# Backward pass of single-query attention: products by streaming evicted blocks past zero-padded columns, scores turned by transposes

## The chip, the cores and the metric

The kernel runs on one core of a Trainium2 chip. A core has TensorE (PE in the profile, with its weight loads as PEld), VectorE (DVE), ScalarE (ACT), GpSimd (POOL) and SyncE (SP), and 16 DMA engines that move data between HBM and the on-chip memories SBUF and PSUM. The metric is the device time of one execution in microseconds (us), as the median of several runs.

## The reference

For each of 2 x 32 = 64 heads there is one query row q of 128 elements, 8192 key rows and 8192 value rows of 128 elements, all bf16. The function returns the attention output and the gradients of q, k and v for a given grad_out:

```python
def _fwd_reference(q, k, v):
    scale = q.shape[-1] ** -0.5
    scores = jnp.einsum("bhqd,bhkd->bhqk", q, k) * scale
    p = _softmax(scores, axis=-1)
    return jnp.einsum("bhqk,bhkd->bhqd", p, v)
...
    _out, _vjp = jax.vjp(_f, q, k, v)
    _grads = _vjp(grad_out)
```

Written out for one head: s = K q, P = softmax(scale s), out = P V, dP = V grad_out, dS = P (dP - sum(P dP)), dq = scale dS K, dK = scale dS q^T, dV = P grad_out^T. K and V (2 MB each) are read once, dK and dV (2 MB each) are written once.

## The kernel before, in words

K and V of a head lie in SBUF as tiles kt and vt of 128 partitions by 64 blocks of 128 elements: partition p holds 64 consecutive tokens. Five heads have buffers at a time. dV is computed in place over vt, dK over kt, and both are stored from there.

The order of all work is written out by hand (`manual_schedule`, L353 to L399): each engine executes its instructions in program order. A pass of the loop over h works on two heads: y, head h, whose scores are computed, and x, head p = h - 1, whose sums and outer products follow. A pass has eight stages j, each with two halves u. Stages 0 to 3 go over K's blocks of head h, stages 4 to 7 over V's.

- `transposes` (L106): per half, eight PE transposes (matmuls against an identity, L113) put eight 128x128 blocks into one of two PSUM buffers tp; one instruction evicts them to SBUF as ev, on ACT (L120), or on DVE (L118) in the second halves of stages 0 and 7.
- `products` (L124): per half, eight matmuls with an ev block as weights and the one column q (or grad_out) of the head as the moving operand (L136). Each gives 128 scores in a column of `sm` (or `dp`). Products of a half stand one stage behind its transposes.
- `row_max`, `all_max`, `exps` (L158 to L182): the maximum over all scores, through one small PE transpose and a broadcasting matmul, and E = exp(...) on ACT.
- `deltas`, `sums`, `weights` (L191 to L232): the sums of E and of E dP, by a matmul with ones, and from them the weights of the outer products, on DVE.
- `weighted_rows` (L234): the sums over tokens for out and dq, as matmuls of 32 weight columns against 512 streamed elements, four at a time on four column groups of PE (`tile_position`, L241). Eight zero-padded weight tiles wz, one for each of four heads and both sums, place a head's result in its own rows of `acc`; every fourth head `acc_to_sbuf` and `combine` read it.
- `outer` (L266): eight DVE multiplications a head (L271) write dV and dK in place; `store` (L328) issues the 2 MB stores from ACT's queue at stages 4 and 7, and `load` (L97) the loads from SP's queue. One store in 26 goes out in pieces through POOL's queue (L289). The last head's stores are four pieces of 1 MB.

The schedule around the change reads:

```python
            for j in range(NS):
                for u in range(2):
                    if y:
                        transposes(h, j, u)
...
                    if y and j:
                        products(h, j - 1, u)
                    elif x and j == 0:
                        products(p, NS - 1, u)
                    if x and j < 4:
                        weighted_rows(p, j // 2, (2 * (j % 2) + u,))
```

Of the kernel before, what the change touches and what calls it, by code (L numbers as in the profile page):

```python
# [23 lines left out]
def kernel(  # L24
# [34 lines left out]
    for g in range(1, 4):  # L59
# [21 lines left out]
    qT_all = const.tile([P, BH], BF16)  # L81
    doT_all = const.tile([P, BH], BF16)


    rl_all = const.tile([P, 2, BH], F32)

    wz = [
        [const.tile([P, NT // 4, 32], BF16, name=f"wz{w}{k}") for k in range(OG)]
        for w in range(2)
    ]  # L90
    colsT = const.tile([P, 2, BH], BF16)
# [5 lines left out]
    def load(h):  # L97
        x = heads[h]
        x.kv = [
            kvp.tile([P, NT, D], BF16, name="kt", tag="kt"),  # L100
            kvp.tile([P, NT, D], BF16, name="vt", tag="vt"),
        ]
        for dst, src in zip(x.kv, (k_v, v_v)):
            nc.sync.dma_start(out=dst[:], in_=src[h])

    def transposes(h, j, u):  # L106

        x = heads[h]
        w, c = divmod(j, NS // 2)
        tp = ps_tp.tile([P, HC, P], F32, name="tp", tag="tp")  # L110
        for i in range(HC):
            n = c * CH + u * HC + i
            nc.tensor.matmul(  # L113
                tp[:, i, :], lhsT=x.kv[w][:, n, :], rhs=ident_bf[:], start=True, stop=True
            )
        ev = evp.tile([P, HC, P], BF16, name="ev", tag="ev")
        if u and j in (0, 7):
            nc.vector.tensor_copy(out=ev[:], in_=tp[:])  # L118
        else:
            nc.scalar.copy(out=ev[:], in_=tp[:])  # L120
        x.ev = getattr(x, "ev", {})
        x.ev[j, u] = ev

    def products(h, j, u):  # L124
        x = heads[h]
        w, c = divmod(j, NS // 2)
        if c == 0 and u == 0:
            if w:
                x.dp = ps_one.tile([P, NT + 2], F32, name="dp", tag="dp")
            else:  # L130
                x.sm = ps_one.tile([P, NT + P + 1], F32, name="sm", tag="sm")
        ev = x.ev.pop((j, u))
        col = (qT_all, doT_all)[w][:, h : h + 1]
        for i in range(HC):
            n = c * CH + u * HC + i
            nc.tensor.matmul(  # L136
                (x.dp if w else x.sm)[:, n : n + 1], lhsT=ev[:, i, :], rhs=col,
                start=True, stop=True,
            )

# [17 lines left out]
    def row_max(x):  # L158
        x.mp = work.tile([P, 1], F32, name="mp", tag="mp")
        nc.vector.reduce_max(out=x.mp[:], in_=x.sm[:, 0:NT], axis=AX.X)  # L160

    def all_max(x):
        mT = x.sm[0:1, NT : NT + P]
# [4 lines left out]
    def exps(x):  # L168
        mb = x.sm[:, NT + P : NT + P + 1]
# [6 lines left out]
            out=x.E[:],  # L176
            in_=x.sm[:, 0:NT],
# [6 lines left out]
    def to_weights(h, w, src):  # L184
        k = h % OG
        nc.vector.tensor_copy(  # L186
            out=wz[w][k][:, :, 16 * w + 4 * k : 16 * w + 4 * k + 4],
            in_=src[:].rearrange("p (m j) -> p m j", j=4),
        )

    def deltas(x):  # L191
        junk = work.tile([P, NT], BF16, name="junk", tag="junk")
        nc.vector.tensor_tensor_reduce(  # L193
            out=junk[:],
            in0=x.E[:],
            in1=x.dp[:, 0:NT],
# [7 lines left out]
    def sums(x):  # L204
        x.lsum = x.dp[:, NT : NT + 2]
        nc.tensor.matmul(x.lsum, lhsT=ones_f[:], rhs=x.ld[:], start=True, stop=True)  # L206

    def weights(h):
        x = heads[h]
        rl, rls = rl_all[:, 0, h : h + 1], rl_all[:, 1, h : h + 1]  # L210
        nc.vector.reciprocal(out=rl, in_=x.lsum[:, 0:1])  # L211
        negdelta = work.tile([P, 1], F32, name="negdelta", tag="negdelta")
        nc.vector.tensor_scalar(
            out=negdelta[:], in0=x.lsum[:, 1:2], scalar1=rl, scalar2=-1.0,
            op0=ALU.mult, op1=ALU.mult,
        )
        nc.vector.tensor_scalar(out=rls, in0=rl, scalar1=scale, scalar2=None, op0=ALU.mult)
        dSu = work.tile([P, NT], F32, name="dSu", tag="dSu")
        nc.vector.scalar_tensor_tensor(
            out=dSu[:], in0=x.dp[:, 0:NT], scalar=negdelta[:], in1=x.E[:],  # L220
            op0=ALU.add, op1=ALU.mult,
        )
        to_weights(h, 1, dSu)

        x.w2 = []
        for name, src, s in (("P2", x.E, rl), ("dS2", dSu, rls)):
            t = work.tile([P, NT, 2], BF16, name=name, tag=name)
            nc.vector.tensor_scalar(
                out=t[:], in0=src[:].unsqueeze(2).to_broadcast([P, NT, 2]),
                scalar1=s, scalar2=None, op0=ALU.mult,  # L230
            )
            x.w2.append(t)  # L232

    def weighted_rows(h, w, chunks):  # L234


        rows, k = heads[h].kv[1 - w], h % OG
        for c in chunks:
            for g in range(4):
                n = c * CH + 4 * g  # L240
                nc.tensor.matmul(  # L241
                    acc[32 * g : 32 * g + 32, :],
                    lhsT=wz[w][k][:, n // 4, :],
                    rhs=rows[:, n : n + 4, :].rearrange("p n d -> p (n d)"),
                    start=(w == 0 and k == 0 and c == 0),
                    stop=(w == 1 and k == OG - 1 and c == NT // CH - 1),
                    tile_position=(0, 32 * g),
                )
# [5 lines left out]
    def combine(h):  # L254

        x = heads[h]
        c = ps_one.tile([P, 2, OG], F32, name="c", tag="c")
        for j in range(4):
            nc.tensor.matmul(  # L259
                c[:], lhsT=x.accsb[:, j * D : (j + 1) * D], rhs=pick[:, j],  # L260
# [3 lines left out]
        nc.vector.tensor_mul(out=colsT[:, :, own], in0=c[:], in1=rl_all[:, :, own])  # L264
# [75 lines left out]
    spare = const.tile([16, 1024], BF16)  # L340
# [4 lines left out]
    for w in range(2):  # L345
        for t in wz[w]:
            nc.gpsimd.memset(t[:], 0.0)
    for src, dst in ((nat[:, 0, :], qT_all), (nat[:, 1, :], doT_all)):
        tps = ps_tp.tile([P, BH], BF16, name="tps", tag="tp")
        nc.tensor.transpose(tps[:], src, ident_bf[:BH, :BH])  # L350
        nc.vector.tensor_copy(out=dst[:], in_=tps[:])

    with tc.manual_schedule():  # L353
        for h in range(min(UNITS, BH)):
            load(h)
        for h in range(BH + 1):
# [4 lines left out]
            for j in range(NS):  # L361
                for u in range(2):
                    if y:
                        transposes(h, j, u)
                    if u == 0:
                        if x and j == 1:
                            sums(x)
                        if y and j == 5:
                            all_max(y)
                        if y and j == 6:  # L370
                            exps(y)
                    if y and j:
                        products(h, j - 1, u)
                    elif x and j == 0:
                        products(p, NS - 1, u)
                    if x and j < 4:
                        weighted_rows(p, j // 2, (2 * (j % 2) + u,))
                if x and j == 0:
                    deltas(x)
                if x and j == 1:  # L380
                    weights(p)
                if y and j == 4:
                    row_max(y)
                if y and j == 7:
                    to_weights(h, 0, y.E)
                if x and p < BH - 1 and j in (4, 7):
                    store(p, j // 7)
                if x:
                    for i in ((), (0,), (1, 2), (3, 4), (5,), (6,), (7,), ())[j]:
                        outer_and_store(p, i // 4, i % 4)  # L390
                    if full and j == 4:
                        acc_to_sbuf(x)
                    if full and j == 6:
                        combine(p)
                if j == 7:
                    if x and UNITS <= h + 3 < BH:
                        load(h + 3)
                    if y and h % QG == 0:
                        spread_rows(h // QG)  # L399
# [37 lines left out]
```

## Time and profile before

| what | value |
|---|---|
| median of 3 runs | 1285.84 us (1284.8 to 1286.18) |
| profiled execution, span | 1285.1 us |
| PE busy, weight loads PEld | 1060.3 us (83%), 877.3 us (68%) |
| DVE busy | 883.8 us (69%) |
| ACT busy | 909.3 us (71%) |
| POOL busy | 105.8 us (8%) |
| DMA | 539.69 MB, mean 420 GB/s |
| PE instructions | 18948 matmuls, 18948 weight loads |

The profile is of one execution, whose span is 1285.1 us; the device time of the runs includes a little around a span. Busy time is the time in which an engine executed something, with overlaps of pipelined matmuls counted once. A line of a group or of the timeline names the source line, the engine, the operation, the tile that is written and those that are read, their shape, and in brackets how long the engine had been idle and who released it. In a line of a stretch, the pairs are busy time and number of instructions of PE, PEld, DVE, ACT and POOL; then follow the clock granted to PE, the busy share of the DMA engines and GB/s. Timeline lines give start and length in us.

### The profile page before, as it was taken

What the parts mean: (1) busy time and instruction counts of PE and PEld (TensorE: products, weight loads), DVE (VectorE), ACT (ScalarE), POOL (GpSimd) and SP (SyncE); (2) the same over time, 40 slices, a digit from 0 to 9 for tenths busy, and PEclk for the clock granted to TensorE, in tenths of its full rate; (3) what the DMA queues carried; (4) which work ended last, traced back from release to release, by engine and by line L of the source; (5) the groups of instructions that cost most, each with busy time, mean ns of one, the idle gap of its engine ahead of it and who ended that gap; (6) DMA issues with size and microseconds to landing.
All of it is one profiled execution on the core that took longest, in us unless ns stands there. A gap on an engine that the chain in (4) does not pass through costs nothing.

```text
span 1285.1 us, 42433 instructions
## 1 busy us (share of the span) xinstructions
PE 1060.3 (83%) x18948; PEld 877.3 (68%) x18948; DVE 883.8 (69%) x1511; ACT 909.3 (71%) x1043; POOL 105.8 (8%) x193
## 2 busy tenths in 40 slices
PE   5999888848998799499997984999889849899983
PEld 4777777637777677477776774777767737777772
DVE  1887777737787486378875773787767636778775
ACT  5877778737887586488875774877767736788771
POOL 1000111000002110000021200000111000001120
PEclk9999999969999697799996897998979877999996
DMA  9999999999999999999999999999999999999998
GB/s 396 418 426 428 426 426 425 423 431 427 426 426 426 413 424 427 423 427 425 428 426 399 427 426 418 428 427 428 419 403 426 425 419 391 428 429 425 425 424 336
DMA packets 43879, 539.69 MB, mean 420 GB/s; under 512 B 10192, under 2 KB 10192, under 8 KB 10192
## 3 DMA queue, kind: packets, MB, share of 16 engines
q1 hardware_dynamic: 18432, 268.44, 49.5%
q10 hardware_dynamic: 18320, 258.02, 47.4%
q0 software_dynamic: 6944, 10.51, 2.2%
q8 instruction: 148, 2.42, 0.7%
q14 instruction: 35, 0.29, 0.1%
HBM read 268.47 MB, written 268.47 MB: 418 GB/s over the span
## 4 chain that ended last, share of the span: by engine, by line
PE 40%; DMA 26%; ACT 19%; DVE 11%; issue 3%; ACTq 0%; DVEq 0%; SPq 0%
PE tp L113 23%; ACT ev L120 18%; DMA vt<-in_v_dram 9%; DVE ev L118 9%; DMA out_dram<-vt 9%; PE acc L241 9%; DMA kt<-in_k_dram 4%; PE sm L136 4%; DMA out_dram<-kt 3%; PE dp L206 1%; PE dp L136 1%; PE c L259 1%; DMA nat<-in_grad_out_dram 1%; ACT E_f L175 1%; PE sm L170 1%
## 5 line engine op out<-in xcount | busy, mean ns | idle before, releaser
L120 ACT CAST ev<-tp 128x1024 bf16<-128x1024 f32 x896 | 881.2, 1024 | 335.7 <-PE tp L113 232.3
L113 PE MATMUL tp<-ident_bf,vt 128*128 128x128 bf16 x4096 | 327.4, 225 | 134.7 <-ACT ev L120 121.6
L113 PEld LDWEIGHTS <-vt 128*128 128x128 bf16 x4096 | 268.9, 100 | 167.3 <-issue 153.2
L113 PE MATMUL tp<-ident_bf,kt 128*128 128x128 bf16 x4096 | 335.9, 228 | 17.2 <-DMA kt<-in_k_dram 6.5
L113 PEld LDWEIGHTS <-kt 128*128 128x128 bf16 x4096 | 249.4, 101 | 131.5 <-issue 123.2
L136 PEld LDWEIGHTS <-ev 128*128 128x128 bf16 x8192 | 324.4, 98 | 2.2 <-issue 0.2
L271 DVE TENSOR_TENSOR kt<-qd,dS 128x2048 bf16<-128x2048 bf16 x256 | 310.0, 1212 | 0.0
L271 DVE TENSOR_TENSOR vt<-qd,P 128x2048 bf16<-128x2048 bf16 x256 | 295.8, 1216 | 0.0
L118 DVE CAST ev<-tp 128x1024 bf16<-128x1024 f32 x128 | 156.7, 1224 | 186.4 <-PE tp L113 179.4
L136 PE MATMUL dp<-doT_all,ev 128*128 128x1 bf16 x4096 | 178.5, 164 | 0.1
L136 PE MATMUL sm<-qT_all,ev 128*128 128x1 bf16 x4096 | 176.0, 164 | 0.0
L299 POOL DMA_DIRECT2D out_dram<-vt x120 | 67.0, 560 | 1032.7 <-DVE vt L271 832.1
L241 PE MATMUL acc<-vt,wz 128*32 128x512 bf16 x1024 | 109.3, 418 | 17.8 <-DVE wz L186 17.8
L241 PE MATMUL acc<-kt,wz 128*32 128x512 bf16 x1024 | 103.4, 396 | 0.1
L172 DVE TENSOR_SCALAR negm<-sm 128x1 f32<-128x1 f32 x64 | 9.8, 154 | 108.8 <-PE sm L170 108.8
L241 PEld LDWEIGHTS <-wz 128*32 128x32 bf16 x2048 | 52.8, 93 | 32.1 <-DVE wz L186 22.7
L285 POOL DMA_DIRECT2D spare<-in_q_dram x57 | 34.1, 598 | 121.1 <-DMA out_dram<-vt 107.0
L206 PE MATMUL dp<-ld,ones_f 128*128 128x2 f32 x128 | 25.8, 271 | 21.0 <-DVE ld L193 20.9
L206 PEld LDWEIGHTS dp<-ld,ones_f 128*128 128x128 f32 x128 | 20.6, 202 | 31.1 <-DVE ld L193 31.0
L160 DVE TENSOR_REDUCE mp<-sm 128x1 f32<-128x64 f32 x64 | 14.4, 225 | 36.9 <-PE sm L136 36.9
L211 DVE RECIPROCAL rl_all<-dp 128x1 f32<-128x1 f32 x64 | 10.7, 168 | 32.0 <-PE dp L206 32.0
L170 PE MATMUL sm<-gm,ones_f 1*128 1x1 f32 x128 | 25.8, 268 | 0.0
(42 smaller groups left out, 310.5 us busy)
## 6 DMA issues: line engine op xcount, KB each, us to landing
kt<-in_k_dram SPq DMA_DIRECT2D x64, 2048.0 KB, 22.9
vt<-in_v_dram SPq DMA_DIRECT2D x64, 2048.0 KB, 31.5
out_dram<-kt ACTq DMA_DIRECT2D x63, 2048.0 KB, 26.9
out_dram<-vt ACTq DMA_DIRECT2D x58, 2048.0 KB, 21.9
out_dram<-vt POOLq DMA_DIRECT2D x20, 176.0 KB, 23.2
out_dram<-vt POOLq DMA_DIRECT2D x40, 64.0 KB, 23.0
out_dram<-vt POOLq DMA_DIRECT2D x20, 128.0 KB, 22.6
out_dram<-vt ACTq DMA_DIRECT2D x2, 1024.0 KB, 10.9
```

Of the source, the lines that this page charges most:

```text
L113: nc.tensor.matmul(tp[:, i, :], lhsT=x.kv[w][:, n, :], rhs=ident_bf[:], start=True, stop=True)
L118: nc.vector.tensor_copy(out=ev[:], in_=tp[:])
L120: nc.scalar.copy(out=ev[:], in_=tp[:])
L136: nc.tensor.matmul((x.dp if w else x.sm)[:, n : n + 1], lhsT=ev[:, i, :], rhs=col, start=True, stop=True,)
L160: nc.vector.reduce_max(out=x.mp[:], in_=x.sm[:, 0:NT], axis=AX.X)
L170: nc.tensor.matmul(mb, lhsT=ones_f[0:1, :], rhs=x.gm[:], start=True, stop=True)
L175: nc.scalar.activation(out=x.E[:], in_=x.sm[:, 0:NT], func=ACT.Exp, bias=negm[:], scale=scale, accum_out=x.ld[:, 0:1],)
L206: nc.tensor.matmul(x.lsum, lhsT=ones_f[:], rhs=x.ld[:], start=True, stop=True)
L241: nc.tensor.matmul(acc[32 * g : 32 * g + 32, :], lhsT=wz[w][k][:, n // 4, :], rhs=rows[:, n : n + 4, :].rearrange("p n d -> p (n d)"), sta ...
L271: nc.vector.tensor_tensor(out=x.kv[1 - w][:, n : n + CH, :].rearrange("p n (d t) -> p n d t", t=2), in0=row.unsqueeze(1).to_broadcast([P, ...
L285: nc.gpsimd.dma_start(out=two(spare[0:n, :])[:, :, i : i + 2], in_=two(q_rows[0:n, :])[:, :, 0:2])
L299: nc.gpsimd.dma_start(out=dst[own], in_=src[own], max_dma_last_dim=size)
```

## The change

- The evicted blocks become the moving operand, and the column of q (or grad_out) the weights. Four matmuls a stage, one for each of PE's four column groups, each stream four blocks (512 elements) past four weight columns, three of which are zeros: q stands in column 3 of its four in `qz`, and the slice that is taken begins 3 - c columns to the left, so that the products of stage c land in row c of the group's four rows of `raw`, where four stages accumulate.
- So the products of both halves of a stage run together, once, behind the first half of the next stage.
- `raw` (512 scores in each of 16 rows) is copied to SBUF by DVE and turned by four fp32 transposes on PE into `turned`, where the scores stand by token again: for K at stages 4 and 5 of the head's own pass, for V at stages 0 and 1 of the next.
- The sum of E and the sum of E dP become two matmuls, the first at stage 7 of the head's own pass; `weights` splits into `weights_v` (stage 7) and `weights_k` (stage 1 of the next pass).
- One wz tile with 60 columns for each of the two sums takes the place of four with 32 columns; a shifted slice of it gives the head's rows.
- DVE evicts the second halves of stages 6 and 7, not of 0 and 7. Outer products, stores (stages 3 and 6), the second sum, `spread_rows` and `combine` move in the schedule.

The diff, cut to its core:

```diff
@@ transposes, products
-            n = c * CH + u * HC + i
+            n = CH * (2 * u + i // 4) + 4 * c + i % 4
...
-        if u and j in (0, 7):
+        if u and j in (6, 7):
             nc.vector.tensor_copy(out=ev[:], in_=tp[:])
         else:
             nc.scalar.copy(out=ev[:], in_=tp[:])
...
-    def products(h, j, u):
+    def products(h, j):
         x = heads[h]
         w, c = divmod(j, NS // 2)
...
-        ev = x.ev.pop((j, u))
-        col = (qT_all, doT_all)[w][:, h : h + 1]
-        for i in range(HC):
-            n = c * CH + u * HC + i
+        at = 4 * h + 3 - c
+        evs = [x.ev.pop((j, u)) for u in range(2)]
+        for k in range(4):
             nc.tensor.matmul(
-                (x.dp if w else x.sm)[:, n : n + 1], lhsT=ev[:, i, :], rhs=col,
-                start=True, stop=True,
+                raw[32 * k : 32 * k + 4, :],
+                lhsT=qz[w][:, at : at + 4],
+                rhs=evs[k // 2][:, 4 * (k % 2) : 4 * (k % 2) + 4, :].rearrange("p n d -> p (n d)"),
+                start=(c == 0),
+                stop=(c == NS // 2 - 1),
+                tile_position=(0, 32 * k),
             )
+
+    def raw_to_sbuf(x):
+        x.raw = work.tile([P, 4 * P], F32, name="rawsb", tag="rawsb", bufs=1)
+        nc.vector.tensor_copy(out=x.raw[:], in_=raw[:])
+
+    def turn_scores(x):
+        out = turned[:].rearrange("p (z i) -> p i z", i=4)
+        for i in range(4):
+            nc.tensor.transpose(out[:, i], x.raw[:, i * P : (i + 1) * P], ident_f[:])
+
+    scores = turned[:].rearrange("p (k z) -> p k z", k=4)[:, :, 0:16]
...
+    def sums(x, w):
+        x.lsum = misc[:, 16 + 8 * w : 17 + 8 * w]
+        nc.tensor.matmul(x.lsum, lhsT=ones_f[:], rhs=x.ld[:, w : w + 1], start=True, stop=True)
...
+    def weighted_rows(h, w, c):
+        rows, k = heads[h].kv[1 - w], h % OG
+        at = 28 - 16 * w - 4 * k
+        for g in range(4):
+            n = c * CH + 4 * g
+            nc.tensor.matmul(
+                acc[32 * g : 32 * g + 32, :],
+                lhsT=wz[w][:, n // 4, at : at + 32],
...
@@ schedule
+    SUM_V = ((0, 0), (0, 1), (1, 0), (1, 1))
+    SUM_K = ((2, 1), (3, 0), (3, 1), (4, 0))
+    OUT = ((0,), (1,), (2, 3), (4, 5), (6,), (7,), (), ())
...
                     if u == 0:
...
                         if y and j == 6:
                             exps(y)
-                    if y and j:
-                        products(h, j - 1, u)
-                    elif x and j == 0:
-                        products(p, NS - 1, u)
-                    if x and j < 4:
-                        weighted_rows(p, j // 2, (2 * (j % 2) + u,))
-                if x and j == 0:
-                    deltas(x)
+                        if y and j:
+                            products(h, j - 1)
+                        elif x and j == 0:
+                            products(p, NS - 1)
+                        if y and j == 5:
+                            turn_scores(y)
+                        if x and j == 1:
+                            turn_scores(x)
+                        if y and j == 7:
+                            sums(y, 0)
+                    else:
+                        if x and j == 1:
+                            sums(x, 1)
+                        if full and j == 6:
+                            combine(p)
+                    if x:
+                        for w, when in enumerate((SUM_V, SUM_K)):
+                            if (j, u) in when:
+                                weighted_rows(p, w, when.index((j, u)))
+                    if u == 0:
+                        if x and j == 0:
+                            raw_to_sbuf(x)
+                        if y and j == 4:
+                            raw_to_sbuf(y)
+                        if x and j == 1:
+                            deltas(x)
+                        if y and j == 5:
+                            row_max(y)
+                if y and j == 5:
+                    all_max(y)
+                if x and p < BH - 1 and j in (3, 6):
+                    store(p, j // 6)
+                if x:
+                    for i in OUT[j]:
+                        outer_and_store(p, i // 4, i % 4)
+                    if full and j == 5:
+                        acc_to_sbuf(x)
                 if x and j == 1:
-                    weights(p)
-                if y and j == 4:
-                    row_max(y)
+                    weights_k(x)
                 if y and j == 7:
-                    to_weights(h, 0, y.E)
-                if x and p < BH - 1 and j in (4, 7):
-                    store(p, j // 7)
...
+                    weights_v(h)
...
+                if y and j == 4 and h % QG == 0:
+                    spread_rows(h // QG)
```

## The prediction

> **What bounds the kernel now.** I read the page first (engines, queues), then the stretches, the waits, and the timeline of one slot. A slot is one pass of the loop over h: eight stages j, each of two halves u; a half is eight transposes on PE and one eviction ev.
>
> ```profile
> DMA  9999999999999999999999999999999999999998
> q1 hardware_dynamic: 18432, 268.44, 49.5%
> q10 hardware_dynamic: 18320, 258.02, 47.4%
> q0 software_dynamic: 6944, 10.51, 2.2%
> q8 instruction: 148, 2.42, 0.7%
> ```
>
> The 16 DMA engines are busy in every slice; loads (q1) and stores (q10) take 97% of their time. PE (83%), ACT (71%) and DVE (69%) are not full. The stretches show why:
>
> ```profile
> 40.00:240.00 200.00, 179.28 (x3364) 148.86 (x3362) 156.38 (x266) 160.76 (x187) 19.95 (x35) 1.00 1.01 424
> 240.00:280.00 40.00, 19.32 (x311) 15.98 (x308) 13.65 (x24) 15.91 (x18) 0.00 (x0) 0.72 1.01 429
> 280.00:400.00 120.00, 108.74 (x2035) 89.81 (x2033) 95.99 (x164) 95.98 (x110) 4.53 (x8) 0.99 1.01 427
> ```
>
> PE (first pair of numbers), DVE and ACT (third and fourth) run, stand still for some 27 us in 240:280, and run again, while the DMA share (last but one) stays at 1.01. So the engines are faster than the DMA and wait for it. How much faster is in the timeline: the transposes that open a slot start at 350.17 and 367.46, so a slot that waits for no transfer takes 17.3 us, 18.1 where spread_rows stands in it, 17.5 in the mean. The DMA needs (1283 - 2)/64 = 20.0 us per head (first packet at 2, last at 1283). **The cover of every change to PE, ACT and DVE is this 2.5 us per slot.**
>
> ```profile
> 343.33 1.01 ACT L120 CAST ev<-tp 128x1024 bf16<-128x1024 f32 x1
> 344.39 0.61 PE L113 MATMUL tp<-ident_bf,vt 128*128 128x128 bf16 x8 [0.28 <-ACT ev L120]
> 344.83 0.27 PE L164 MATMUL sm<-ident_f,mp 128*1 128x128 f32 x1
> 344.94 0.34 PE L136 MATMUL dp<-doT_all,ev 128*128 128x1 bf16 x8
> 352.14 0.34 PE L136 MATMUL dp<-doT_all,ev 128*128 128x1 bf16 x8
> 352.41 0.40 PE L241 MATMUL acc<-vt,wz 128*32 128x512 bf16 x4
> 352.74 0.62 PE L113 MATMUL tp<-ident_bf,kt 128*128 128x128 bf16 x8
> 353.45 1.01 ACT L120 CAST ev<-tp 128x1024 bf16<-128x1024 f32 x1 [1.57 <-PE tp L113]
> ```
>
> Read here: an eviction ends at 344.34 and the transposes that reuse its buffer start 0.05 later; the eviction of transposes begun at 352.74 starts 0.71 later; eight old products take 0.27 of PE (352.14 to 352.41); four L241 matmuls on four column groups take 0.33 (352.41 to 352.74), though each is listed at 390 ns, so they overlap.
>
> **The change, part by part.** *PE work.* Out: 128 products a head, in 16 groups of 0.27 = 4.3 us. In: 8 groups of four matmuls 128x4 by 512; the nearest row is L241's, 0.33 each = 2.6. In: eight fp32 transposes a head in two groups. One alone is L164: 0.27 listed, but the next matmul starts 0.11 later; eight fp32 passes of L259 take 1.04, or 0.13 each. A group of four lies between 4 x 0.11 = 0.44 and 4 x 0.273 = 1.1; I take 0.52, L259's spacing, since its weights are fp32 128x128 as here. The sums are done twice (+0.26, from L206). In total PE is the same within 0.4 us and not full.
>
> *Order, the dear part.* Before, a half's products come behind its transposes and need an older eviction, so the second half's transposes start as soon as the last second-half eviction frees their buffer. After, products run once a stage, ahead of the second half's transposes, and need both evictions of the stage before. PE executes in order, so from one second-half eviction to the next there is now a loop that nothing overlaps: wake 0.05, products 0.33, transposes to eviction 0.71, eviction 1.01 (L120), together 2.10. Queued behind the waiting products are these transposes, and ACT waits for them. Per slot:
> - eight loops: 16.8
> - two of the eight evictions are on DVE (stages 6 and 7), 1.22 instead of 1.01: +0.4
> - weighted sums that stand ahead of second-half transposes (stages 0, 1, 3, 4): 4 x 0.33 = 1.3
> - turn_scores ahead of them (stages 1 and 5): 2 x 0.52 = 1.0
> - the row-sum matmul at stage 7: 0.26
> - spread_rows, 0.5 in one slot of four: 0.1
>
> Sum **19.9 us per slot** against 17.5. Its bounds: where one column-group matmul follows another (stages 0, 3, 4) the first may take 0.25, if the 0.1 of weight loads (L241's PEld row) hides (-0.24), and transposes may go at 0.11 (-0.2): 19.4 below. Transposes at twice L259's spacing give 20.9 above.
>
> A page rule on this: the Trainium skill, TensorEngine Tiling (Array Packing), section Tiling Modes, says that changing the tiling mode drains the engine. The trace agrees: the weight load behind each L241 group sits idle 0.23 us, and this is inside my 0.33. By the rule a drain stands ahead of each group too, at most 8 x 0.23 = 1.8 us more per slot; I count none, since products wait for an eviction there anyway.
>
> *Hidden.* raw_to_sbuf: two copies of 0.68 (L252, same shape) on DVE; the first reader of raw's next round is a stage, over 2 us, away. DVE comes to 13.8 + 1.4 = 15.2 of 19.9, ACT stays at 15. If DVE ran late by more than a microsecond, that lateness would be added. The maximum's chain (row_max, its transpose, exps) ends ahead of stage 6's products, which wait for an eviction longer. Fewer memsets and the smaller spare: nothing. The transfers keep their sizes, queues and order, POOL's included; only the stores are issued a stage earlier, which helps little while DMA has a backlog.
>
> *Instruction fetch.* PE's 37,896 instructions become 26,888 (counted in the program, fp32 in two passes). q8's 2.42 MB over 37,896 is 64 B each, so 43 of its 148 packets of 16 KB go. At 0.7% of 16 x 1285 us over 148, a packet costs 0.97 us of an engine: 42 us in all, or 2.6 us if spread over 16 engines. In the packet records, q8's durations repeat in eights and about half of the engines end at 1276, the rest by 1283, so I take it that eight engines carry it: up to 5.2 us less where the DMA bounds.
>
> *Sum.* The first transposes start at 12.0; 64 x 19.9 = 1273.6; from there, in the last slot, 1.5 until the last eviction, 0.4 products, 0.7 copy, 0.3 deltas, eight outer products at 1.16 (L271 in a row) = 9.3, weights 1.0: 13.2 to the last store; its 1 MB at 427 GB/s 2.5, and 2.0 from the last packet to the end of the span (1283.1 to 1285.1): 1303.3. Waits for late transfers come on top, since DMA then also works at 98%: 0 (its backlog shrinks) to 10 (a third of the 27 us stop); I take 2. The profiled span of before, 1285.1, lies 0.7 under the median of its runs, 1285.84. **1306 us.**
>
> **The rivals.** *The DMA stays the bound, the fetch shrinks (faster).* If the slot takes under 19.4, the last store is issued before the DMA's backlog ends, and only the fetch counts: 1285.8 - 2.6 to 5.2 = 1280.6 to 1283.2, so 1281. What speaks for it: the slot is a sum of eight like loops, and 0.06 less in each is enough. Against it: each term is read from a row, and none overlaps. The point of decision: 12 + 64s + 17.7 + 0.7 + 2 = 1285.8 gives s = 19.6.
>
> *Both cancel*: s between 19.5 and 19.6, 1283.5 to 1288.
>
> *The transposes do not overlap*: eight of 0.273 instead of 0.13, 1.1 us more per slot, plus 64 x 1.1: 1379. Beside this row stands the Trainium skill, TensorE: Matmul & The Clock Gate, Part 4, with about 275 ns for a 128x128 transpose in a kernel; the 8 bf16 transposes here go at 0.06 us each, so the trace does not bear it out as a spacing.
>
> *The column groups don't overlap for four weight columns*: four streams of 512 at the transposes' pace (128 columns in 0.055) take 0.88 instead of 0.33, 8 x 0.55 = 4.4 per slot, 1588. L241's overlap with 32 columns speaks against it.
>
> **How the numbers follow.** Forecast 0.59; DMA-bound 0.26; cancelled 0.07; slow transposes 0.06; serial groups 0.02. The range runs from the DMA-bound time to s = 20.5 (1345), leaving out the two dearest and the tails. About 0.2% is what a measurement can tell from no change: faster than that 0.26, within 0.07, slower 0.67.
>
> **What would show it.** Right: DMA share falls under 1 in most stretches, the long stops of PE and ACT vanish, a slot takes 19.5 to 20.5, and transposes of second halves follow the product group. q8 shows 105 packets. Wrong: stops of 20 us stay and slots between them take under 19.4 (DMA-bound); L148's four take over 1 us; L131's four take over 0.8. Waits of products for raw's copy would mean that DVE is late, which I cost at nothing.

## The result and the profile after

The changed kernel takes **1296.19 us** (median; 1295.57 to 1300.16) against 1285.44 us for the kernel before on the same chip (1284.8 to 1286.18): a ratio of 1.0089, 95% interval 1.0074 to 1.0105 (ratios are quoted as recorded; the quotient of the two medians is 1.0084). It is slower, by 10.7 us; 1306 was forecast, in a range of 1280 to 1345.

First the engines, the DMA and the instruction queue on the page of the changed kernel:

```profile
span 1294.5 us, 31642 instructions
PE 1171.5 (91%) x13444; PEld 726.1 (56%) x13444; DVE 970.1 (75%) x1640; ACT 912.5 (70%) x1043; POOL 104.1 (8%) x189
DMA  9999999999999999999999999999999999999976
q1 hardware_dynamic: 18432, 268.44, 49.1%
q10 hardware_dynamic: 18320, 258.02, 47.1%
q8 instruction: 105, 1.72, 0.5%
```

PE has 5504 matmuls fewer and is busy 111 us longer. q8 carries 105 packets instead of 148, as counted beforehand. The DMA engines are full up to the last two of 40 slices and not in those. The stretches of the changed kernel (PE, PEld, DVE, ACT, POOL; granted clock, DMA share, GB/s) show the two things to look for:

```profile
40.00:240.00 200.00, 185.10 (x2144) 114.16 (x2138) 154.45 (x259) 144.61 (x166) 19.89 (x35) 1.00 1.01 418
240.00:280.00 40.00, 37.20 (x432) 23.17 (x429) 30.87 (x53) 29.24 (x34) 0.00 (x0) 1.00 1.01 427
280.00:400.00 120.00, 110.40 (x1274) 68.25 (x1272) 91.14 (x154) 86.33 (x100) 0.00 (x0) 1.00 1.01 427
...
1240.00:1280.00 40.00, 34.96 (x399) 21.02 (x397) 31.68 (x56) 25.19 (x30) 5.68 (x10) 1.00 0.63 260
1280.00:1294.00 14.00, 3.51 (x26) 2.30 (x26) 7.88 (x10) 0.52 (x2) 0.00 (x0) 0.53 0.73 302
```

The stop in 240:280 is gone (37.20 us of PE work instead of 19.32). At the end the kernel before has this line:

```profile
1240.00:1280.00 40.00, 23.59 (x376) 17.37 (x372) 26.22 (x44) 15.81 (x20) 5.69 (x10) 0.76 0.96 401
```

There the DMA was kept at 0.96; in the changed kernel it stands at 0.63: the transfers wait for PE. How one stage now runs is in the timeline, around the change from V's last stages to the next head's first:

```profile
601.93 1.22 DVE L120 CAST ev<-tp 128x1024 bf16<-128x1024 f32 x1 [1.32 <-PE tp L115]
...
602.20 0.38 PE L131 MATMUL raw<-ev,qz 128*4 128x512 bf16 x2
...
603.21 0.38 PE L131 MATMUL raw<-ev,qz 128*4 128x512 bf16 x2 [0.62 <-DVE ev L120]
...
603.31 0.49 PE L256 MATMUL acc<-vt,wz 128*32 128x512 bf16 x4
...
603.74 0.62 PE L115 MATMUL tp<-ident_bf,kt 128*128 128x128 bf16 x8
...
604.45 1.93 ACT L122 CAST ev<-tp 128x1024 bf16<-128x1024 f32 x2 [1.07 <-PE tp L115]
```

The first two products (602.20) need only the first half's eviction; the other two stop PE for 0.62 us until DVE has evicted the second half (601.93 + 1.22 = 603.15). Behind them stand a weighted group and the next second half's transposes (603.74), and behind those ACT, which had waited 1.07 us when it starts at 604.45. This is the loop of the prediction.

**Where the 9.4 us between the two profiled spans lie** is read from the transposes that open a slot. Slot 53 is the first behind the last long stop, slot 63 the last full one. In the timeline of the kernel before they start here:

```profile
1063.12 1.01 PE L113 MATMUL tp<-ident_bf,kt 128*128 128x128 bf16 x8 [0.23 <-DVE ev L118]
...
1241.49 0.61 PE L113 MATMUL tp<-ident_bf,kt 128*128 128x128 bf16 x8
```

and in that of the changed kernel here:

```profile
1058.95 0.61 PE L115 MATMUL tp<-ident_bf,kt 128*128 128x128 bf16 x8
...
1254.91 0.61 PE L115 MATMUL tp<-ident_bf,kt 128*128 128x128 bf16 x8
```

Up to slot 53 the changed kernel is 4.2 us *ahead*; over ten slots it takes 196.0 instead of 178.4, 17.6 more; from slot 63 to the end 39.6 instead of 43.6, 4.0 less. 17.6 - 4.2 - 4.0 = 9.4. These are two single executions; the experiments show how far two executions of one kernel can lie apart up to slot 53 (e9).

### The profile page after: what moved, and what is told of

Its sections match the earlier page's. It is cut to its first block, busy times and chain, and to the rows that moved or that the text cites. A ratio compares the mean times of both kernels' runs of the same rounds, so it can differ in the third digit from the quotient of the medians.

```text
span 1294.5 us, 31642 instructions
## 1 busy us (share of the span) xinstructions
PE 1171.5 (91%) x13444; PEld 726.1 (56%) x13444; DVE 970.1 (75%) x1640; ACT 912.5 (70%) x1043; POOL 104.1 (8%) x189
## 5 line engine op out<-in xcount | busy, mean ns | idle before, releaser
L131 PE MATMUL raw<-ev,qz 128*4 128x512 bf16 x2048 | 354.9, 379 | 81.9 <-DVE ev L120 61.8
L115 PE MATMUL tp<-ident_bf,vt 128*128 128x128 bf16 x4096 | 304.9, 220 | 9.1 <-ACT ev L122 9.1
L115 PEld LDWEIGHTS <-vt 128*128 128x128 bf16 x4096 | 251.5, 99 | 74.5 <-issue 67.6
L131 PEld LDWEIGHTS <-qz 128*4 128x4 bf16 x2048 | 83.7, 81 | 248.1 <-issue 195.4
L256 PE MATMUL acc<-kt,wz 128*32 128x512 bf16 x1024 | 126.0, 387 | 1.1 <-DVE wz L203 1.1
L142 DVE COPY rawsb<-raw 128x512 f32<-128x512 f32 x128 | 88.4, 690 | 12.5 <-PE raw L131 10.2
L148 PE MATMUL turned<-ident_f,rawsb 128*128 128x128 f32 x512 | 84.4, 288 | 0.4 <-DVE rawsb L142 0.4
L256 PEld LDWEIGHTS <-wz 128*32 128x32 bf16 x2048 | 52.5, 93 | 34.2 <-issue 10.7
L148 PEld LDWEIGHTS turned<-ident_f,rawsb 128*128 128x128 f32 x512 | 53.9, 141 | 29.9 <-issue 29.1
L200 PEld LDWEIGHTS misc<-ld,ones_f 128*128 128x128 f32 x256 | 38.4, 189 | 15.1 <-ACT ev L122 10.7
L200 PE MATMUL misc<-ld,ones_f 128*128 128x1 f32 x256 | 45.9, 249 | 0.3 <-DVE ld L227 0.3
```

What stands on the lines that cost most here:

```text
L115: nc.tensor.matmul(tp[:, i, :], lhsT=x.kv[w][:, n, :], rhs=ident_bf[:], start=True, stop=True)
L131: nc.tensor.matmul(raw[32 * k : 32 * k + 4, :], lhsT=qz[w][:, at : at + 4], rhs=evs[k // 2][:, 4 * (k % 2) : 4 * (k % 2) + 4, :].rearrange ...
L142: nc.vector.tensor_copy(out=x.raw[:], in_=raw[:])
L148: nc.tensor.transpose(out[:, i], x.raw[:, i * P : (i + 1) * P], ident_f[:])
L200: nc.tensor.matmul(x.lsum, lhsT=ones_f[:], rhs=x.ld[:, w : w + 1], start=True, stop=True)
L256: nc.tensor.matmul(acc[32 * g : 32 * g + 32, :], lhsT=wz[w][:, n // 4, at : at + 32], rhs=rows[:, n : n + 4, :].rearrange("p n d -> p (n d)"),
```

## The experiments

Theory: the order makes the slot longer (products ahead of the second half's transposes wait for an eviction). Rivals: the turning of the scores or the streamed products themselves are dear; or the slot is not what sets the end. Slots are quoted as the mean of four that wait for no transfer (one of the four holds spread_rows): 17.50 before, 19.65 after.

**e1_products_later** undoes the order alone, in the changed kernel:

```diff
-                    if u == 0:
+                    if u == 1:
                         if y and j:
                             products(h, j - 1)
...
-                    if u == 0:
+                    if u == 1:
                         if x and j == 0:
                             raw_to_sbuf(x)
```

(the sum at stage 7 goes with them; turn_scores, deltas and row_max stay at u == 0.)

> The changed kernel with products and the copy of raw moved behind the second half's transposes; the same instructions, another order. Theory A (the loop: products ahead of the second half's transposes hold these back until an eviction is done): the loop loses 0.33 us in each of eight stages and the waits for the copy, the slot falls from 19.4 to about 17.5 to 18, the DMA bounds again, stops of PE and ACT return, and the time is 1280 to 1283 us, the DMA-bound time with the smaller instruction fetch. Rival B (PE is full, with its drains at each change between whole and four-column-group matmuls): the work and the changes are the same, the slot stays at 19 or more, and the time stays at 1290 to 1296.

Measured: **1276.82 us** (1276.49 to 1277.1), ratio to before 0.9921, 0.9907 to 0.9935; a second run of the same kernel on another chip (e9, below) gave the same ratio. The time is 3 us under the range I gave. Slot 17.58. The streamed products, the turning and the second sum all remain, so none of them by itself makes the slot longer; the order does. The stops are back, and the instruction queue is as short as in the changed kernel. From the stretches of e1:

```profile
40.00:240.00 200.00, 184.72 (x2377) 122.50 (x2377) 169.79 (x289) 161.15 (x186) 19.97 (x35) 1.00 1.01 426
240.00:280.00 40.00, 18.17 (x218) 12.19 (x215) 14.95 (x25) 14.99 (x17) 0.00 (x0) 0.74 1.01 431
```

This version beats both kernels.

**e2_products_and_sum_later** is e1 with one more group moved: `SUM_V = ((0, 1), (1, 0), (1, 1), (2, 0))`.

> As the run before, and the first weighted sum moved half a stage later too, so that it no longer waits for E's weights ahead of stage 0's second-half transposes. Theory A: another 0.3 us off the slot at stage 0; as the DMA already bounds, the time stays at 1280 to 1283, the same as the run before within 0.2%. Rival B: slot 19 or more, 1290 to 1296.

Measured: 1276.86 us (1275.99 to 1278.22), ratio 0.9922, 0.9909 to 0.9935. The shorter slots (regular ones of 17.04 instead of 17.25) bring nothing measurable: the transfers bound.

**e3_turn_twice** prices the turning, in the changed kernel: the four transposes are issued twice with the same values.

```diff
-        for i in range(4):
+        for i in (0, 1, 2, 3, 0, 1, 2, 3):
             nc.tensor.transpose(out[:, i], x.raw[:, i * P : (i + 1) * P], ident_f[:])
```

> The changed kernel with turn_scores' four transposes issued twice (the second four write the same values again). The time of four is 0.5 to 0.6 us. Theory A: they stand in the loop at stages 1 and 5, so the slot grows by 1.0 to 1.15 us and the time by 64 times that: 1360 to 1370 us. If instead the DMA set most of the time of the changed kernel (19.65 us per slot against 20.0 per head), the first 0.4 us per slot would cost nothing and the time would be 1330 to 1345.

Measured: 1347.41 us (1346.65 to 1347.84), ratio 1.0471, 1.0454 to 1.0488, between the two ranges that I gave; regular slots of 20.32 instead of 19.45. So a group of four costs 0.87 / 2 = 0.44 us, not the 0.5 to 0.6 that I expected, and the time follows the slot (51 us for 64 x 0.87 = 56; the changed kernel waits for a transfer in slot 52, 25.06 us instead of its regular 20.49, and e3, with 21.37 there, does not): with slots above the transfers' pace the kernel is PE's from end to end. A line of e3's groups shows that a longer listed duration is not the spacing, 280 ns for one that costs 110:

```profile
L148 PE MATMUL turned<-ident_f,rawsb 128*128 128x128 f32 x1024 | 139.8, 280 | 0.4 <-DVE rawsb L142 0.4
```

**e4_half_products** takes instructions away from the kernel before: every second product is left out and the others write two columns, so half of the scores are not computed.

```diff
-        col = (qT_all, doT_all)[w][:, h : h + 1]
-        for i in range(HC):
+        two = min(h, BH - 2)
+        col = (qT_all, doT_all)[w][:, two : two + 2]
+        for i in range(0, HC, 2):
...
-                (x.dp if w else x.sm)[:, n : n + 1], lhsT=ev[:, i, :], rhs=col,
+                (x.dp if w else x.sm)[:, n : n + 2], lhsT=ev[:, i, :], rhs=col,
```

> The kernel before with every second product left out (each remaining matmul writes two columns, so half of the scores are wrong); 8192 PE instructions fewer, 32 packets of instruction fetch of 16 KB, and less PE work. It prices the rival of the prediction: with the DMA as the bound and PE faster still, only the fetch can count. 32 x 0.97 us spread over 16 engines is 1.9 us less, over eight engines 3.9 us less: 1281.5 to 1283.5 us. If the fetch does not count, 1285.4, the same within 0.1%.

Measured: 1278.59 us (1277.77 to 1279.75), ratio 0.9936, 0.9924 to 0.9949. Its queue line, against 148 packets before:

```profile
q8 instruction: 116, 1.90, 0.5%
```

32 packets fewer and 8.1 us; e1 has 43 fewer and 9.8 us (1286.65 - 1276.82). If the packets were all that counts, each would cost 0.25 and 0.23 us. I had expected 0.06 to 0.12. The next three runs ask whether it is the packets.

**e5_three_tiny** and **e6_one_wide** add instructions to e1, behind each half's transposes, whose results nothing reads:

```diff
+        for i in range(3):
+            nc.tensor.matmul(
+                misc[0:1, 300 + i : 301 + i], lhsT=ident_bf[:, 0:1], rhs=ident_bf[:, 0:1], start=True, stop=True
+            )
```

in e5, and in e6

```diff
+        nc.tensor.matmul(
+            misc[0:1, 300:428], lhsT=ident_bf[:, 0:1], rhs=ident_bf[:], start=True, stop=True
+        )
```

> The kernel of e1_products_later, with three extra matmuls of one column by one column behind each half's transposes, into an unused corner of misc; nothing reads their results. They add 6144 instructions to PE's 25,114 (24 packets of 16 KB on q8, so 129 instead of 105) and little work; the slots between stops should stay under 19, so that the transfers still bound. Price theory: an instruction packet costs 0.23 to 0.25 us of the whole time, as the 32 packets of e4_half_products and the 43 of e1_products_later have it; then 24 packets bring 5.5 to 6.0 us more than e1's 1276.8, about 1282.5. Rival: the gains of e1 and e4 came in part from something else (fewer gaps of the transfers), and a packet costs 0.06 to 0.12 us as I had estimated; then 1278.3 to 1279.7.

> The kernel of e1_products_later, with one extra matmul of one column by 128 behind each half's transposes, whose result nothing reads: about as much work on PE as the three tiny ones, but a third of the instructions (2048, 8 packets, 113 in all). Price theory: 8 x 0.23 to 0.25 = 1.8 to 2.0 more than e1, about 1278.7, and some 3.8 under e5_three_tiny. Rival of cheap packets: 1277.3 to 1277.8, and 1 to 2 under e5. If the work and not the number of instructions counts, e5 and e6 come out alike.

**e7_later_turn_twice** is e1 with e3's edit.

> The kernel of e1_products_later with the four turn transposes issued twice, the same edit that cost 51 us on top of the changed kernel (1347.4 against 1296.2). Theory: in e1 the slots between stops take 17.25 us against the transfers' 20, so about 0.9 us more per slot is covered, and only the 2048 further instructions count (8 packets): 1277.3 to 1278.8. Rival: if PE's work set the end in e1 too, or if the cover were smaller than the 2.5 us by which I reckon it, part of 50 us comes back: over 1290.

Measured, on one chip with 1286.88 before:

| kernel | packets | slot | us (lowest to highest) | ratio |
|---|---|---|---|---|
| e5 | 129 | 18.59 | 1287.88 (1285.48 to 1292.13) | 1.0008 (0.9993 to 1.0023) |
| e6 | 113 | 18.42 | 1283.75 (1280.17 to 1293.43) | 0.9988 (0.9965 to 1.001) |
| e7 | 109 | 18.44 | 1283.22 (1280.29 to 1289.99) | 0.9977 (0.9956 to 0.9998) |

e5 and e6 lie above what either theory gave, e7 above the theory's and far under the rival's. e7 has four packets more than e1 and takes 6 us more: something other than packets counts, and it goes with the slot, though the mean slot is well under the transfers' 20. Its twelve runs are far apart (seven of 1280.3 to 1283.7, five of 1288.1 to 1290.0, the profiled one among these), so the 6 us are rough. They are not e3's 51, so most of the cover is there, but not all of it. e6 lies 4.1 under e5 with 16 packets fewer (3.8 were expected), and between e5 and e7 20 packets stand against 4.7 us, 0.23 each once more. Of both, some 1.5 us can come from the slots, which differ by 0.15 to 0.17 in ten slots behind the last stop (see below). With these spreads that agrees with the price and does not prove it. The stretch 1240:1280 shows where e5 loses, first in the line of e5 itself:

```profile
1240.00:1280.00 40.00, 29.59 (x416) 19.43 (x413) 33.66 (x54) 20.83 (x25) 6.31 (x11) 0.91 0.80 331
```

The DMA share is 0.80, where the kernel before has 0.96; in 1240:1260 it is 0.81, and 0.93 in e1: at the end even these slots come too late.

**e8_pool_adds** was to add e5's 6144 instructions on POOL, off the slot; **e9_products_later_again** is e1 unchanged beside it.

```diff
+                        for i in range(6):
+                            nc.gpsimd.tensor_tensor(out=junk[:], in0=junk[:], in1=junk[:], op=ALU.add)
```

> The kernel of e1_products_later with six additions of eight numbers per half on POOL, which is idle 92% of the time in e1; nothing reads their results. They add 6144 instructions (24 packets on q8, 129 instead of 105), as e5_three_tiny does, but not one to PE, so that the slot should stay at 17.25 and the last slot's compute should not end later. Price theory: 0.23 to 0.25 us for each packet wherever it is fetched, 5.5 to 6.0 more than e9_products_later_again of the same call. Rival: of the 11 us that e5 lay above e1, most came from PE's longer slots, above all the last one, which no transfer covers (the DMA share falls to 0.81 in 1240:1260 of e5, 0.93 in e1); then a packet costs 0.06 to 0.12 and this is 1.4 to 2.9 more than e9.

> The kernel of e1_products_later unchanged, as the basis of e8_pool_adds on the same chip, and to learn whether e1's 0.9921 of before holds on another chip: 1276 to 1278 by both theories.

Measured: e9 1277.23 us (1276.9 to 1285.28), ratio 0.9921, 0.9904 to 0.9937; e8 2243.66 us, ratio 1.7428, 1.7399 to 1.7457. e8 failed as an experiment. Its group and queue lines tell why:

```profile
L392 POOL TENSOR_TENSOR junk<-junk 1x8 f32<-1x8 f32 x6144 | 1640.2, 267 | 482.8
```

```profile
q8 instruction: 105, 1.72, 0.3%
q14 instruction: 84, 0.69, 0.1%
```

An addition of eight numbers, each on the result of the one before, is listed at 267 ns, and 79 more go by ahead of it (482.8 / 6144), 2123 us in all; POOL became the bound, and the stores behind it on its queue came late. Nor did q8 grow: q14 went from 36 packets in e1 to 84, 8 KB for each further packet, so POOL's instructions do not come by the queue I meant to load.

**e10_sums_later** leaves the changed kernel's products where they are and moves the four weighted groups that stand ahead of second-half transposes behind them: `SUM_V = ((0, 1), (0, 1), (1, 1), (1, 1))`, `SUM_K = ((2, 1), (3, 1), (3, 1), (4, 1))`. **e11_old_products_earlier** brings the new order alone into the kernel before:

```diff
+                    for v in range(2) if u == 0 else ():
                         if y and j:
-                            products(h, j - 1, u)
+                            products(h, j - 1, v)
                         elif x and j == 0:
-                            products(p, NS - 1, u)
+                            products(p, NS - 1, v)
```

> The changed kernel, products ahead of the second half's transposes as in it, but all eight groups of weighted sums behind the second half's transposes. Theory of the prediction (in the loop from one second-half eviction to the next everything ahead of the transposes counts): the four groups that stood ahead go out of the loop, 4 x 0.33 = 1.3 us less per slot, from 19.45 to about 18.1, under the transfers' 20, so the DMA bounds again: 1277 to 1282. Rival (in stages 0, 1, 3 and 4 PE is simply full, whatever the order): the slot stays at 19.2 to 19.5 and the time at 1288 to 1297.

> The kernel before with its 16 old products issued together once a stage, ahead of the second half's transposes: the order of the changed kernel without its streamed products and without the scores' way over raw and turned. Theory: the same loop, with 0.27 instead of 0.33 for the group of eight that waits: 8 x (0.05 + 0.27 + 0.71 + 1.01) = 16.3, two evictions on DVE 0.4, four weighted groups 1.3, spread_rows 0.1: a slot of about 18.1 instead of 17.3; the transfers still bound, so 1284 to 1289. Rival (the order costs nothing by itself, the turning and the waits for both evictions do): the slot stays at 17.3 and the time at 1285 to 1288.

Measured, with 1286.59 before: e10 1284.75 us (1282.56 to 1289.0), ratio 0.9985, 0.9966 to 1.0003; e11 1294.95 us (1291.52 to 1298.33), ratio 1.0052, 1.0031 to 1.0074. Both slots answer as the loop says: e10's falls from 19.65 to 18.71 (0.94 for four groups, against 1.3 by my count and 0 by the rival), e11's rises from 17.50 to 18.77 without streamed products and without turning. Both times are above what I expected. Part of e11's is the clock; its stretches, one line for each slot:

```profile
1040.60:1060.50 19.90, 17.38 (x306) 13.79 (x306) 15.66 (x27) 14.36 (x17) 0.00 (x0) 1.00 1.01 428
...
1079.40:1099.80 20.40, 18.73 (x293) 14.19 (x293) 13.63 (x23) 13.88 (x16) 0.00 (x0) 0.83 1.00 425
1099.80:1120.20 20.40, 18.72 (x294) 14.24 (x294) 13.64 (x24) 13.88 (x16) 0.00 (x0) 0.83 1.01 430
...
1159.70:1178.30 18.60, 16.26 (x294) 12.64 (x294) 13.63 (x23) 13.78 (x16) 0.00 (x0) 1.00 1.00 423
```

With the same 294 matmuls a slot takes 18.6 us at a granted clock of 1.00 and 20.4 at 0.83. The ten slots from 53 on take 196.3 us instead of 10 x 18.77, 8.6 lost so. e10 has no such slots there, and is still 8 us above e1.

**What e5 to e10 have in common** is that the time rises long before the slot reaches the transfers' 20 us. Set side by side, in the profiled executions:

| kernel | slot | slot 53 starts | slots 53 to 63 | slot 63 to the end | span |
|---|---|---|---|---|---|
| e4 | 16.83 | 1055.0 | 183.1 | 38.7 | 1276.8 |
| before | 17.50 | 1063.1 | 178.4 | 43.6 | 1285.1 |
| e1 | 17.58 | 1056.0 | 179.7 | 39.5 | 1275.2 |
| e9, the kernel of e1 | 17.58 | 1062.9 | 183.3 | 37.0 | 1283.2 |
| e6 | 18.42 | 1059.3 | 184.0 | 37.7 | 1281.0 |
| e7 | 18.44 | 1064.0 | 184.5 | 39.2 | 1287.8 |
| e5 | 18.59 | 1060.9 | 187.2 | 37.9 | 1286.0 |
| e10 | 18.71 | 1056.3 | 186.4 | 38.6 | 1281.3 |
| after | 19.65 | 1059.0 | 196.0 | 39.6 | 1294.5 |
| e3 | 20.53 | 1099.4 | 204.9 | 40.6 | 1344.9 |

Up to slot 53 the start does not follow the slot, as long as it stays under 20: it lies between 1055.0 and 1064.0 in no order of the slots, and the kernel of e1 alone gives 1056.0 and 1062.9 (e9 was profiled in the longest of its six runs, 1285.28). What is gained is stood idle, most of it in the stops at slots 13, 26, 39 and 52: in the kernel before 71 of 124 us above 53 slots of 17.50, in e1 83 of 112. In the kernel before all four begin at ACT: with a store of dV next in its queue and evictions behind that, it waits 15.0 to 17.3 us (63.9 in all), which the profile puts down to loads of V that land at the end of each wait; why the store is held so long is not shown. Behind the last stop come ten slots that go nearly at PE's pace, but for slot 60 of e1, e4 and e9, which has such a wait once more (23.6 us in e1, where slots of its kind take 18.8). So a theory of its own: the changed order is paid for in the last eleven heads alone. **e12_last_heads_later** tests it, with the changed kernel's order up to slot 52 and e1's from 53 on:

```diff
+            late = 1 if h >= 53 else 0
...
-                    if u == 0:
+                    if u == late:
                         if y and j:
                             products(h, j - 1)
...
-                    if u == 0:
+                    if u == late:
                         if x and j == 0:
                             raw_to_sbuf(x)
```

> The changed kernel as it is for the slots 0 to 52, and the order of e1_products_later (products, sums and raw_to_sbuf behind the second half's transposes) from slot 53 on, eleven of the 64 heads. Theory: slot 53 starts at 1055 to 1064 in the profiles of every kernel so far whose slots stay under 20 (1063.1 before, 1059.0 in the changed kernel, 1056.0 in e1, 1056.3 in e10_sums_later), since up to there the transfers bound, with stops of 21 to 40 that make good any difference; only the ten slots behind the last stop and the 39 us from slot 63 to the end run at PE's pace. So the changed order costs its time only there, and this kernel gets it back nearly whole: 1059.0 + 10 x 17.98 (e1's mean there) + 39.4 + 1.9 outside the span = 1280, with 1277 to 1282 as the range. Rival: a longer slot costs the same anywhere, because the transfers' backlog, once lost, is lost; then the gain is 11/64 of the 19.4 us between the changed kernel and e1: 1293.

Measured: **1282.2 us** (1280.25 to 1287.45), ratio 0.9963, 0.9947 to 0.9978, 0.2 above my range and 11 under the rival's 1293. Of the 19.4 us between the changed kernel and e1, 14.0 come back by another order in eleven of 64 heads. In the timeline of e12 slots 52, 53 and 63 start here:

```profile
1033.34 0.61 PE L115 MATMUL tp<-ident_bf,kt 128*128 128x128 bf16 x8
...
1056.57 0.61 PE L115 MATMUL tp<-ident_bf,kt 128*128 128x128 bf16 x8
...
1241.28 0.61 PE L115 MATMUL tp<-ident_bf,kt 128*128 128x128 bf16 x8
```

Slots of 19.44 up to 52, as in the changed kernel, and slot 53 within 0.6 us of e1's; then 184.7 us for ten instead of 196.0. That includes slot 60 with 27.8, where ACT waits 7.4 us ahead of a store of dV (3.0 in e1). Of the 4.8 us between the two profiled spans of e12 and e1, 4.2 lie in this slot (27.8 against 23.6); why its store is held longer is not shown.

## Why the prediction was right, and where it was not

- **The mechanism, right.** Products ahead of the second half's transposes close a loop that nothing overlaps. e1 opens it and the slot falls from 19.65 to 17.58; e11 closes it in the kernel before and the slot rises by 1.27.
- **The slot, 19.9: 0.25 too long.** Over 64 slots this is 16.0 us, more than the whole error, and the next item takes back 5.2 of it, which is luck. The mis-sized terms: the four weighted groups, 1.3, cost 0.94 (e10). Where one stands behind products that wait, the group ahead of it adds 0.10 in place of 0.33 (603.21 to 603.31), since its first two matmuls had run at 602.20, and the weighted group itself 0.43 (603.31 to 603.74); I had counted that as a lower bound (0.25) and not far enough. A turning group is 0.44 by e3, not 0.52. spread_rows costs 1.05 (20.49 instead of 19.44) in one slot of four, not 0.5 (in the kernel before, too, its slot takes 18.59, not the 18.1 of the prediction). Together these take 0.4 off, so 0.1 the other way is left in terms that no run took apart. A drain of 0.23 ahead of each column group as well would, by my estimate, have made the slot up to 21.7, and it takes 19.65. The Trainium skill, TensorEngine Tiling (Array Packing), section Tiling Modes, says that a change of the tiling mode drains the engine. What the changed kernel's timeline shows ahead of such a group is 0.1 us: eight transposes take 0.55 to the start of products (585.18 to 585.73) and 0.46 where a sum follows (587.30 to 587.76).
- **The start, the late transfers and the tail: 5.2 too short together.** First transposes at 12.5 instead of 12.0. Waits for transfers: slot 63 would start at 12.5 + 63 x 19.65 = 1250.5 and starts at 1254.9, so 4.4 instead of 2. (The stop of the kernel before in 240:280, of which I took a third as the bound, is 17.5 us of PE and not 27: PE waits from 257.5 to 274.99.) From the end of the 64th slot (1254.9 + 19.65) to the end of the span 20.0 instead of 17.7. With the slots: 12.5 + 1257.6 + 4.4 + 20.0 = 1294.5, the span; my terms gave 1305.3.
- **"PE is the same within 0.4 us": right of the work, wrong in the profile's terms.** Busy time went up by 111 us (83% to 91%). But e1, with the same instructions in another order, is busy 1065.6 us, 5.3 more than before: the products (L131) are listed at 200.8 us there and at 354.9 in the changed kernel. So the rise is the order's; that it is time spent waiting for evictions inside the groups is my reading of it.
- **The engines behind it, right.** DVE is at 75%, its copies of raw take 0.69 and hold PE up for 0.4 us in all: L131's waits are for evictions (61.8 us for DVE's, nearly all the rest for ACT's), as the group lines of the changed kernel have it:

```profile
L131 PE MATMUL raw<-ev,qz 128*4 128x512 bf16 x2048 | 354.9, 379 | 81.9 <-DVE ev L120 61.8
L148 PE MATMUL turned<-ident_f,rawsb 128*128 128x128 f32 x512 | 84.4, 288 | 0.4 <-DVE rawsb L142 0.4
```

- **The slow transposes and the serial column groups, rightly put low.** Four turning transposes take 0.44, not 1.1, and products of four column groups take about 0.33 where they don't wait for an eviction, as this timeline of e1 has it (0.36 to the next transposes, 0.31 to the next sum):

```profile
607.19 0.39 PE L131 MATMUL raw<-ev,qz 128*4 128x512 bf16 x4
607.55 0.61 PE L115 MATMUL tp<-ident_bf,vt 128*128 128x128 bf16 x8
...
609.19 0.39 PE L131 MATMUL raw<-ev,qz 128*4 128x512 bf16 x4
609.50 0.38 PE L200 MATMUL misc<-ld,ones_f 128*128 128x1 f32 x2
```

- **The fetch: foreseen in packets, its time not shown.** 43 packets of 148 went as counted. I took them at 2.6 to 5.2 us, and only for the rival in which the DMA bounds. e1, which is that rival made real, gained 9.8, e4 8.1 for 32. No run showed that the packets are the cause of all of it. In the packet records of the profiled executions all packets together take 1283.3 us of each of the 16 engines before, 1276.4 in e1 and 1277.6 in e4. q8's own packets, with a mean of 0.95 us, are 2.5 and 1.9 us of these 6.9 and 5.7; more of it, 3.7 and 2.9, comes from the load packets, which are as many and as large but shorter in the mean (552.5 ns before, 549.3 in e1, 550.0 in e4). The changed kernel, with 105 packets too, has 552.2. What shortens them is open; e1 also issues its stores a stage earlier, which e4 does not.
- **The point of decision, 19.6: wrong in form.** I set the sum of slots against the DMA's end, with one sharp point between them. The runs show a bend instead: 18.44 costs some 6 us against e1 (e7), 18.71 costs 8 (e10), 19.65 costs 19.4. The step that failed is "cover of 2.5 us per slot": most of the idle time lies in four stops, and behind the last, at slot 52, ten slots and the tail have little of it. That this did not spoil the time is luck: at 19.65 a slot is as long as the transfers' own pace up to there ((1059.0 - 12.5) / 53 = 19.75), so that both ways of counting meet.
- **One sign did not come.** The DMA share was to fall under 1 in most stretches. It stays at 1.00 or 1.01 in nearly all of them up to 1240, though the stops are gone, since PE's slots and the transfers are about equally long there; it falls only at the end (0.63).
- **Put together**, the change is +19.4 us of order (e1 to after) and -9.8 us of everything else (before to e1), for which the fetch is a candidate, not shown. That gives +9.6 against the 10.7 measured; the two kernels ran on different chips, on which the kernel before took 1286.65 and 1285.44, and the difference between these is the rest.

## What to carry to other kernels

When an engine works in order, put what waits for an eviction behind the work that starts the next eviction; the same instructions, 2 us of a slot apart, made the difference between 0.8% faster and 0.9% slower. An engine that is idle for a sixth of the span does not have that cover everywhere: look where the stops lie, and take what follows the last one as uncovered. In a kernel whose DMA is full, look at the number of instructions too: their fetch goes by the same 16 engines, and two versions with fewer of them (e1, e4) were 8 to 10 us faster here, though no run showed that the fetch is why.

## What the runs showed of the hardware

- Instructions of PE came on q8 in packets of 16 KB, 64 B each, and those of POOL, in e8, on q14 in packets of 8 KB (6144 further instructions, 48 further packets).
- A POOL addition of eight fp32 numbers on one partition, in a row on one tile, is listed at 267 ns, with 79 ns of idle time ahead of it (e8).
- The granted clock of PE fell to 0.83 in some slots of e11, which is busy 86% with 18,948 matmuls, and stayed at 1.00 in every stretch of 40 us of the changed kernel up to 1280 but one (0.91 in 1040:1080), which is busy 91% with 13,444. Busy time alone does not say when the clock is taken back; what does, these runs leave open.
- fp32 128x128 transposes in a row go at 0.11 us each (0.44 for four, e3), with 280 to 288 ns listed; bf16 ones go at 0.055 us each (eight in 0.44, 601.22 to 601.66 in the changed kernel), with 220 ns listed. The Trainium skill, TensorE: Matmul & The Clock Gate, Part 4, has about 275 ns for a 128x128 bf16 transpose in a kernel; by these rows a figure of that size is the length of one and not the distance between two.
